# q, k and v as interleaved Strassen quads at the front of an attention and gMLP kernel, with all of v at one time

## The chip, the cores and the metric

The kernel runs on one core of a Trainium2 chip. The metric is the device time of one execution in microseconds (us), as the median of several executions. Every run told here was in the fast state. PE is the TensorE matmul engine, DVE is VectorE, ACT is ScalarE, SP is SyncE (which here issues nearly all transfers), POOL is GpSimd. "Granted clock" is the share of its full speed at which TensorE was clocked.

## The reference, cut to what matters

```python
def _A_ref(x, wqkv, wo):                     # S = 2048, D = 1024, H = 32 heads of 32
    W, dil = (8, 2)                          # each position attends to 8 others, two apart
    qkv = (x @ wqkv).reshape(B, S, 3, H, Dh).transpose(2, 0, 3, 1, 4)
    ...
    logits = einsum('bhsd,bhswd->bhsw', q, kg) * scale      # kg, vg: k and v gathered
    attn = softmax(where(mask, logits, -1e9))
    o = einsum('bhsw,bhswd->bhsd', attn, vg)
    return o.transpose(...).reshape(B, S, D) @ wo

def _B_ref(x, w_in, w_sp, b_sp, w_out):      # gMLP: w_in 1024 x 3584, w_sp 2048 x 2048
    z = gelu(x @ w_in);  z1, z2 = halves of z;  z2 = layernorm(z2)
    g = einsum('ts,bsf->btf', w_sp, z2) + b_sp
    return (z1 * g) @ w_out

g = sigmoid((x * gate_w).sum(-1))
return g * _A_ref(x, A_wqkv, A_wo) + (1 - g) * _B_ref(x, ...)
```

## The kernel before

PE works through these stages: transposes of x and the first quarter of z2 (to 35 us), q, k and v with the rest of z2 (to 288 us), then z1, the spatial product and the output product. The 32 heads are eight groups of four. For each group PE makes q and k in eight direct tiles of eight matmuls, and then the band products, q times k near the diagonal. ACT copies the bands out, SP stores them to memory (`band_d`) and loads the 8 logits of every position back (`att_L`), DVE takes the maxima and subtracts them, ACT applies exp, DVE normalises and weighs v. v goes through memory too (`v_d`), because each position needs v of other positions.

```python
def qk_tile(g, t, c):                        # direct: 8 matmuls of 512 columns
    ps = low_bank()                          # one of banks 0 to 3
    for kt in range(KT):
        nc.tensor.matmul(ps[:], w[:, t, kt, :], xT[:, kt, 512 * c:512 * (c + 1)], ...)
    note(nc.scalar.copy(dst[...], ps[:]...))           # counted: evacuation number n

def attend1(g):                              # logits: load, maxima, subtract, exp
    for e in range(2):
        sync.dma_start(L[:, 256 * e:256 * e + 256]..., band_d[g] ...)
    tt(att_m[:], L4[:, :, 0:4, :], L4[:, :, 4:8, :], ALU.max)
    ...
    last_sub[0] = tt(L4, L4, att_m[:, :, 0:1, :].to_broadcast(...), ALU.subtract)
    exps[g] = nc.scalar.activation(L[:], L[:], ACT.Exp, ...)
    # its place in ACT's order: behind evacuation number EXP_AFTER[g]

def weigh(g, e, after=None):                 # half a group: 4.42 + 4.28 us of DVE
    tt(prod..., v_t ..., att_A ..., ALU.mult)
    tt(p3[:, 0:4, :], p3[:, 0:4, :], p3[:, 4:8, :], ALU.add)
    ...                                      # two more additions

for g in range(NG):                          # the main loop
    main = []
    if g == 1: main += [v_tile(0, j) ...]    # first half of v: 16 direct tiles
    if g + 1 < NG: main += [qk_tile(g + 1, t, c) ...]
    else: main += [z2_tile(i, c, low_bank) ...]
    if g == 3: main += [v_tile(1, j) ...]    # second half of v
    ...                                      # three band_sets of g between the tiles (banks 4 to 7)
    if g == 1: load_v(0); weigh(0, 0)
    if g > 0: load_v(g)
    attend1(g)
    if g > 0: weigh(g - 1, 1, last_sub[0])
    attend2(g)                               # sum, reciprocal, att_A
    if g > 0: weigh(g, 0)
```

The later stages use Strassen quads (seven block products in place of eight), two of them interleaved product by product, one on banks 0 to 3 and one on banks 4 to 7. Partial results move from bank to bank by copies, and later products add onto them:

```python
def strassen(A11, A12, A22, S1, ..., T4, vs, c11, c12, c21, c22, share=nc.scalar.copy):
    product(X, zip(A11, B11), True);   nc.scalar.copy(Y[:], X[:])
    yield
    product(V, zip(S1, T1), True);     share(vs, V[:])          # S, T: sums of blocks, by DVE
    yield
    product(Y, zip(S2, T2), False);    nc.scalar.copy(Z[:], Y[:])
    ...                                # products X, Y, Z, V; c22(Y), c12(Z) are DVE additions
```

The order of the instructions on an engine is fixed when the kernel is built. A "NoSync dependency" in the code below fixes such an order without any semaphore.

## Time and profile before

| | before |
|---|---|
| median of 3 runs | 681.91 us (681.83 to 683.17) |
| profiled run | 682.25 us, span 680.2, granted clock 0.999 |
| PE, DVE, ACT busy | 98%, 60%, 43% |
| chain that ended last | PE 95%, DMA 2%, DVE 1% |
| weighing on DVE starts | 102.38 us |
| DVE starts the x differences for z1 | 287.08 us |
| z1 starts on PE (its refresh matmuls: four that write whole banks ahead of the quads that add onto copies in them; 0.86 us in the chain, and no run tried those quads without them) | 288.02 us |
| PE idle for ACT, DVE or a DMA, 30 to 305 us | 0.24 us |

The views themselves, and what is read from them, stand in the prediction below.

### The profile page before, as it was taken

How to read it: one execution, taken by the hardware profiler on the slowest of the kernel's cores; microseconds unless marked ns; L12 is line 12 of the kernel's file. 1: busy time of each engine (PE TensorE's matmuls, PEld its weight loads, DVE VectorE, ACT ScalarE, POOL GpSimd, SP SyncE). 2: the span in 40 equal slices, each digit the busy share in tenths (PEclk: the TensorE clock that was granted, in tenths of full speed). 3: DMA queues.
4: the chain of work that ended last, by engine and by line, in shares of the span. 5: the costliest groups of instructions: out<-in, count | busy, mean ns of one | idle time of the engine just before them, and what ended most of it. 6: DMA issues, size and time to landing. Idle time of an engine off the chain costs nothing.

```text
span 680.2 us, 10313 instructions
## 1 busy us (share of the span) xinstructions
PE 665.4 (98%) x4075; PEld 323.0 (47%) x4135; DVE 407.4 (60%) x551; ACT 289.5 (43%) x547; POOL 6.1 (1%) x15
## 2 busy tenths in 40 slices
PE   6999999999999999999999999999999999999997
PEld 3544654466444555544444444444444444444443
DVE  1000119899199989866769766888676695333301
ACT  4435634624566889677866311212112122222221
POOL 1000000000000000000100000000000000000000
PEclk9999999999999999999999999999999999999999
DMA  9995654764666470138894587648356299944100
GB/s 232 225 277 116 139 137 116 167 172 94 155 177 154 126 163 1 52 104 191 210 187 155 140 195 153 151 129 255 95 149 167 67 208 187 212 106 98 46 32 31
DMA packets 241743, 98.12 MB, mean 144 GB/s; under 512 B 189712, under 2 KB 235168, under 8 KB 241696
## 3 DMA queue, kind: packets, MB, share of 16 engines
q1 hardware_dynamic: 241008, 96.94, 58.2%
q8 instruction: 32, 0.52, 0.3%
q10 hardware_dynamic: 688, 0.53, 0.2%
q14 instruction: 15, 0.12, 0.1%
HBM read 45.10 MB, written 36.61 MB: 120 GB/s over the span
## 4 chain that ended last, share of the span: by engine, by line
PE 95%; DMA 2%; issue 1%; DVE 1%; SPq 1%; ACT 0%; ACTq 0%; DVEq 0%
PE psum_all L474 56%; PE psum_all L272 16%; PE psum_all L232 15%; PE psum_all L280 6%; PE psum_all L312 2%; DMA band_d_71<-arena 1%; DMA arena<-in_A_x_dram 1%; SPq L184 0%; DMA arena<-o_d 0%; DMA v_d<-arena 0%; PE psum_all L202 0%; DVE arena L685 0%; ACT arena L283 0%; DVE arena L680 0%; DVE arena L525 0%
## 5 line engine op out<-in xcount | busy, mean ns | idle before, releaser
L474 PE MATMUL psum_all<-arena 128*128 128x512 f16 (+1 forms) x1758 | 385.6, 379 | 2.0 <-DVE arena L685 0.2
L474 PEld LDWEIGHTS <-arena 128*128 128x128 f16 (+1 forms) x1792 | 175.3, 98 | 212.2 <-issue 1.3
L272 PE MATMUL psum_all<-arena 128*128 128x512 bf16 x493 | 111.0, 379 | 2.3 <-issue 1.9
L232 PE MATMUL psum_all<-arena 128*128 128x448 bf16 (+1 forms) x512 | 99.7, 355 | 0.0
L365 DVE TENSOR_TENSOR arena<-arena,att_A 128x8192 f16<-128x8192 bf16 x16 | 70.7, 4420 | 12.1 <-DMA arena<-v_d 12.0
L272 PEld LDWEIGHTS <-arena 128*128 128x128 bf16 x512 | 48.6, 98 | 56.8 <-issue 0.2
L232 PEld LDWEIGHTS <-arena 128*128 128x128 bf16 x512 | 49.8, 98 | 47.0 <-issue 1.5
L365 DVE TENSOR_TENSOR arena<-arena 128x4096 f16<-128x4096 f16 (+2 forms) x48 | 67.3, 1401 | 1.2
L274 ACT CAST arena<-psum_all 128x512 bf16<-128x512 f32 x64 | 37.4, 586 | 53.3 <-PE psum_all L272 53.3
L280 PE MATMUL psum_all<-arena 128*128 128x512 bf16 x249 | 55.4, 379 | 0.9 <-issue 0.4
L483 ACT COPY psum_all<-psum_all 128x512 f32<-128x512 f32 x36 | 20.5, 570 | 80.7 <-PE psum_all L474 80.7
L523 DVE TENSOR_TENSOR arena<-arena 128x512 f16<-128x512 bf16 (+2 forms) x37 | 20.7, 568 | 42.1 <-PE psum_all L474 30.9
L234 ACT ACTIVATE arena<-psum_all 128x448 bf16<-128x448 f32 x64 | 34.7, 547 | 26.2 <-PE psum_all L232 26.0
L280 PEld LDWEIGHTS <-arena 128*128 128x128 bf16 x256 | 36.7, 144 | 18.5 <-issue 0.5
L497 ACT COPY psum_all<-psum_all 128x512 f32<-128x512 f32 x36 | 20.6, 571 | 48.7 <-PE psum_all L474 48.6
L490 ACT COPY psum_all<-psum_all 128x512 f32<-128x512 f32 x36 | 20.5, 570 | 48.6 <-PE psum_all L474 48.3
L590 ACT ACTIVATE arena<-psum_all 128x512 bf16<-128x512 f32 x56 | 31.6, 599 | 7.2 <-DVE psum_all L593 3.7
L319 ACT CAST arena<-psum_all 128x1988 f16<-128x1988 f32 (+1 forms) x24 | 33.7, 1405 | 1.1 <-PE psum_all L312 0.4
L526 DVE TENSOR_TENSOR arena<-arena 128x512 f16<-128x512 bf16 (+2 forms) x37 | 20.6, 566 | 21.2 <-PE psum_all L474 15.5
L338 DVE TENSOR_TENSOR att_m<-att_L_106 128x256 f16<-128x256 f16 x4 | 1.2, 290 | 50.8 <-DMA att_L_106<-band_d_68 32.8
L283 ACT CAST arena<-psum_all 128x512 bf16<-128x512 f32 x32 | 18.4, 587 | 26.5 <-PE psum_all L280 25.9
L487 ACT COPY arena<-psum_all 128x512 f32<-128x512 f32 x22 | 12.8, 587 | 34.5 <-PE psum_all L474 33.7
(87 smaller groups left out, 361.5 us busy)
## 6 DMA issues: line engine op xcount, KB each, us to landing
arena<-v_d SPq DMA_DIRECT2D x8, 960.0 KB, 6.9
z_d<-arena SPq DMA_DIRECT2D x28, 256.0 KB, 2.6
arena<-z_d SPq DMA_DIRECT2D x28, 256.0 KB, 3.3
zg_d<-arena SPq DMA_DIRECT2D x56, 128.0 KB, 2.2
arena<-zg_d SPq DMA_DIRECT2D x32, 224.0 KB, 3.1
arena<-in_A_wqkv_dram SPq DMA_DIRECT2D x16, 256.0 KB, 5.6
v_d<-arena SPq DMA_DIRECT2D x32, 128.0 KB, 2.4
o_d<-arena SPq DMA_DIRECT2D x4, 1024.0 KB, 5.5
```

Source lines behind the costliest of these rows:

```text
L232: nc.tensor.matmul(ps[:, 0:N], xT[:, kt, i * P:(i + 1) * P], w2[:, kt, w2_off[c]:w2_off[c] + N], start=(kt == 0), stop=(kt == KT - 1))
L234: inst = nc.scalar.activation(z2[:, i, ZC * c:ZC * (c + 1)], ps[:, 0:ZC], ACT.Gelu_apprx_tanh, accum_out=s1[:, 4 * i + c:4 * i + c + 1])
L272: nc.tensor.matmul(ps[:], w[:, t, kt, :], xT[:, kt, 512 * c:512 * (c + 1)], start=(kt == 0), stop=(kt == KT - 1))
L274: inst = nc.scalar.copy(dst[:, :, 256 * c:256 * (c + 1)], ps[:].rearrange("p (n e) -> p e n", e=2))
L280: nc.tensor.matmul(ps[:], _sub_ap(xT_flat, kt * S + j, [[NJ, P]]), wv[:, kt, 512 * hf:512 * hf + 512], start=(kt == 0), stop=(kt == KT - 1))
L319: evac = nc.scalar.copy(dst, src)
L365: inst = nc.vector.tensor_tensor(*a)
L474: nc.tensor.matmul(bank[:], lhsT, rhs, start=(start and m == 0), stop=(stop and m == n - 1), skip_group_check=True)
L497: seed = nc.scalar.copy(V[:], Y[:])
L523: first = nc.vector.tensor_tensor(s_out[0], a21, a22, ALU.add)
L526: nc.vector.tensor_tensor(s_out[2], a11, a21, ALU.subtract)
L590: last_gelu[0] = nc.scalar.activation(z1s[:, f, a, :], bank[:], ACT.Gelu_apprx_tanh)
```

## The change

The intent: 40 fewer matmuls. q and k of groups 0 and 1 become four quads, and 24 of the 32 v tiles become six quads, all at the front, on all eight banks. For that, all of v is made at one time (before: halves in groups 1 and 3), the x differences that the quads need go to buffers that attention uses later, and the places of the exps are counted anew. The eight v tiles of the first two row sets (j = 0 and 1) stay direct, to carry the six band sets of groups 0 and 1 between them.

```diff
-    EXP_AFTER = (20, 27, 51, 60, 83, 93, 103, 117)
+    EXP_AFTER = (7, 10, 22, 33, 43, 53, 65, 78)
...
+    front_x_sums()                       # x differences for the front, on DVE
+    qk_sums(0)
+    refresh([bank_roles[r][y] for r in range(2) for y in (1, 2)])
+    run(qk_quad(0, 0), qk_quad(0, 1))
+    qk_sums(1)
+    run(qk_quad(1, 0), qk_quad(1, 1))
+    wv_sums()
...
+    for m, args in enumerate(tiles):     # 8 direct v tiles, j = 0 and 1
+        for n in range(6):
+            if (0, 1, 3, 4, 5, 7)[n] == m:
+                band_set(n // 3, n % 3)  # bands of group 0, then of group 1
+                if n == 2:
+                    attend1(0)
+        v_tile(*args)
+    refresh(bank_roles[1][1:3])
+    for j in (2, 4, 6):
+        run(v_quad(j), v_quad(j + 1))
+    load_wqk(4, sync.dma_start)
+    for t in range(2):
+        for c in range(4):
+            qk_tile(2, t, c)
+    load_v(0)
+    attend2(0)
+    weigh(0, 0)
+    load_v(1)
+    attend1(1)                           # logits of group 1: maxima, exp
+    weigh(0, 1, last_sub[0])
+    attend2(1)
+    weigh(1, 0)
+    for g in range(2, NG):               # as before, without v
...
```

In the new quads `share` is a DVE copy, so DVE serves each quad with one copy and two additions.

## The prediction

> **What bounds the kernel now.** I read first the page's busy shares, slices and groups.
>
> ```profile
> PE 665.4 (98%) x4075; PEld 323.0 (47%) x4135; DVE 407.4 (60%) x551; ACT 289.5 (43%) x547; POOL 6.1 (1%) x15
> ...
> PE   6999999999999999999999999999999999999997
> ...
> DVE  1000119899199989866769766888676695333301
> ...
> L272 PE MATMUL psum_all<-arena 128*128 128x512 bf16 x493 | 111.0, 379 | 2.3 <-issue 1.9
> ...
> L280 PE MATMUL psum_all<-arena 128*128 128x512 bf16 x249 | 55.4, 379 | 0.9 <-issue 0.4
> ```
>
> TensorE (PE) is busy 98% of a 680.2 us span, 9 or more tenths in every slice but the ends. VectorE (DVE) idles up to about 102 us (zeros and ones, but for one slice), then runs at 8 to 9 tenths. The two groups are the q/k tiles (L272, 64 tiles of 8 matmuls) and the v tiles (L280, 32 of 8). A share of busy time can hide waits, so next what PE waited for, and the chain that ended last:
>
> ```profile
> PE psum_all L202 <- DMA arena<-in_A_x_dram: 5.8, 2, 3.5
> ...
> PE psum_all L280 <- ACT arena L283: 0.2, 1, 0.2
> ```
> ```profile
> 225.90 62.28 PE psum_all L232 x328
> 288.18 0.86 PE psum_all L635 x4
> 289.10 12.03 PE psum_all L474 x55
> 301.18 12.03 PE psum_all L474 x55
> ```
>
> PE loses 5.8 us to the first x loads and hardly anything afterwards; the chain is matmuls back to back. From 289.10 to 301.18 two interleaved seven-product quads (the layer's z1 stage) run: 56 matmuls in 12.08 us, 0.2157 us each. So the existing quads of four matmuls a product already run at PE's full rate with ScalarE (ACT) and DVE serving them. A matmul removed on this path is worth 0.2157 us, provided that nothing else takes its place. The candidate is DVE, whose timeline I read next (start, length, instruction, in brackets the idle time before):
>
> ```profile
> 90.20 0.23 DVE L355 TENSOR_TENSOR att_r<-att_s,g_att 128x64 f16<-128x64 f32 x1
> 102.38 4.42 DVE L365 TENSOR_TENSOR arena<-arena,att_A 128x8192 f16<-128x8192 bf16 x1 [11.96 <-DMA arena<-v_d]
> ...
> 187.65 0.29 DVE L338 TENSOR_TENSOR att_m<-att_L_106 128x256 f16<-128x256 f16 x1 [15.20 <-DMA att_L_106<-band_d_72]
> ...
> 280.46 4.28 DVE L365 TENSOR_TENSOR arena<-arena 128x4096 f16<-128x4096 f16 x3
> 287.08 4.63 DVE L563 TENSOR_TENSOR arena<-arena 128x2048 f16<-128x2048 bf16 x4 [2.35 <-PE psum_all L232]
> ```
>
> The weighing of v (L365) begins when v has come back from memory, at 102.38, and ends about 284.7; DVE waits 2.35 us and starts at 287.08 on x differences for z1, which need the end of the z2 tiles on PE (288.2). So attention on DVE ends with only 2.4 us to spare. Its idle stretches between 102.38 and 284.74, added from this view, are 2.80 + 0.75 + 15.20 + 0.86 + 0.68 + 0.78 = 21.1 us; its work there is 182.4 - 21.1 = 161.3 us, of which about 5.0 us are sums for z1.
>
> [...] before, four full ones stand at 288.18 and take 0.86 us. [...]
>
> ```profile
> L365 DVE TENSOR_TENSOR arena<-arena,att_A 128x8192 f16<-128x8192 bf16 x16 | 70.7, 4420 | 12.1 <-DMA arena<-v_d 12.0
> ...
> L593 DVE TENSOR_TENSOR psum_all<-psum_all,arena 128x512 f32<-128x512 f32 x28 | 18.0, 694 | 10.9 <-ACT psum_all L497 10.9
> ...
> L563 DVE TENSOR_TENSOR arena<-arena 128x2048 f16<-128x2048 bf16 x8 | 9.4, 1221 | 2.3 <-PE psum_all L232 2.3
> ```
>
> 2048 columns from SBUF take 1.22 us, 512 from PSUM 0.69 us.
>
> **The change, part by part.**
>
> PE, removed. q and k of two groups: 16 tiles of 8 matmuls = 128 become 4 quads of 7 products of 4 = 112. v of six blocks: 24 tiles of 8 = 192 become 6 quads of 28 = 168. Together 40 matmuls, 40 x 0.2157 = 8.6 us, all on the path.
>
> PE, added. Two further refreshes, 4 and 2 matmuls, in strips of 32 rows on different parts of the array, so that they may overlap: at most 6 x 0.22 = 1.3 us, my estimate 0.8. The hand-overs between bank users cost more. The tiles rotated through four banks while band products (q times k near the diagonal) used the other four. Now a band set follows a quad on banks 4 to 7 and waits for the quad's last copy (0.59 us plus signalling), a first quad product follows a direct tile on the same bank, and the six band sets of two groups are squeezed between eight tiles. A band evacuation takes 1.82 us on ACT and a tile 1.73 us on PE, so adjacent sets can wait some tenths. I choose 2.3 us for all this. PE so reaches the end of z2 at 288.2 - 8.6 + 0.8 + 2.3 = 282.7 us.
>
> The start. The first quads need wqk of group 0 (issued at 22.9, landing in about 5.6) at 35.3 and the first x difference 1.7 us later. The x differences are 8 x 1.22 = 9.8 us on a DVE that idles from 16 to 36.8 us, and the last x transposes are issued by 22.8 and land in about 4. Only the third difference has a catch: its buffer covers the zeros that are stored to v's border in memory, the last of the start-up loads, whose issue ends at 36.1; it may start near 40 and end at 42.7. Its product comes after eight others of the interleaved pair, at about 42. I count no wait.
>
> ACT and DVE in the quads: per quad of 28 x 0.2157 = 6.04 us ACT has five copies of 0.57 to 0.59 = 2.9 us, DVE three of 0.69 = 2.1 us; over ten quads DVE gets 21 us, and 9.8 us of x differences, 8 x 0.42 = 3.4 of weight sums of q and k and 4 x 1.22 = 4.9 of v. These 39 us lie before 116 us, where DVE had nearly nothing. Beside PE, free.
>
> Moved: all v at one time. From 35.3: four quads 24.2 + 1 us refresh and hand-over, eight direct v tiles 13.8, six band sets 3.7, hand-overs 1.5, six quads 36.2: v is complete at about 115.7 us. Before, its first half was at 94.5:
>
> ```profile
> 94.52 0.59 ACT L283 CAST arena<-psum_all 128x512 bf16<-128x512 f32 x1 [1.14 <-PE psum_all L280]
> 95.13 2.06 SPq L184 DMA_DIRECT2D v_d<-arena  x4
> ...
> 97.30 0.96 SPq L184 DMA_DIRECT2D arena<-v_d  x2
> ```
>
> There the last copy ended at 95.1, small stores (128 KB each) followed, and weighing began 7.3 us after. Now the last store is 1 MB, then the first load of v of 960 KB: at some 200 GB/s (what the page's GB/s row shows in busy slices) 5 us each plus about 1.3 us of issue and latency each, 12.5 us. Weighing begins at 115.7 + 12.5 = 128 us, 26 us later than before. The second v phase inside group 3 disappears, and with it the waits of DVE for group logits (15.2 of the 21.1 us): the logits of groups 2 to 7 now come every 8 x 1.73 + 1.9 = 15.7 us, faster than DVE's 20 us per group. DVE is thus busy without a gap from 128 to 128 + 161.3 = 289.3 us.
>
> The sum. PE is ready for z1 at 282.7, DVE with everything at 289.3. The first z1 products that need a late x difference start some 3.5 us into z1, so at about 287 with 1.22 us of DVE before it. If all attention work stood before those differences, PE would wait about 4 us; but they have a high priority, and part of the last weighing (8.6 us) can come after. It would then be caught up inside z1, where DVE is busy 63.2 of 86 us. I put PE's wait at a third of the full one plus some friction from 4.4 us instructions in front of the quads' additions: 1.0 us. Total: 681.9 - 8.6 + 0.8 + 2.3 + 1.0 = 677.4 us.
>
> **Rivals.**
>
> First: DVE becomes the bound at the join. For it speak 289.3 against 282.7; against it the 27% idle share of DVE in z1. If the queue's order puts all weighing ahead, or v returns 3 us later than thought, PE waits 4 to 7 us and the time is 681 to 684; the gain is gone.
>
> Second: ACT's exps stall PE. They stand at fixed places in ACT's order, and ACT already waited 5.4 us for DVE once (at 148 us), which cost PE only 0.24 us as three more banks were free. With DVE further behind, a wait of 8 us or more would cost PE 3 us at a time in several groups: 684 or more. Against it: the differences of logits that an exp needs are short and come ahead of the weighing in DVE's order.
>
> Third: everything stays hidden and hand-overs cost as little as before: 681.9 - 8.6 + 0.8 = 674.
>
> Fourth: the quads at the front stall for the zeros' store or for wqk: 2 to 4 us more, 680.
>
> **Range and chances.** The gain is capped near 8 us, 1.2%; for 2% (668.3) there are no matmuls. A loss of 2% (695.5) would need several stalls at once. I take 672.8, the third rival with a little luck, to 683 for the first. Faster by over 2%: 0.02; within 2%: 0.95; slower by over 2%: 0.03.
>
> **What would show it.** PE matmul count down by some 34, refreshes counted; the quads at the front taking 12.1 us a pair; weighing beginning near 128 us and running with no gap over 1 us; the end of z2 near 282.7; then the number to look for, PE's wait for DVE in the first z1 pair, about 1 us, and leftover weighing inside z1. It would be wrong if PE stalls in the front's quads, if exps hold ACT for over 6 us, or if z1 starts more than 3 us late.

## The result

The kernel after took 690.22 us (median of 4, 689.39 to 693.58; a fifth fast run, 690.55, counts in the ratio). Before had a median of 682.54 us over 4 runs, the three of the table above and one of 686.91. The ratio is 1.0107, with a 95% interval of 1.0061 to 1.0154; the width comes mostly from that fourth run (against it alone the ratio would be 1.006, against the first three 1.012). Ratios here are the mean time of one kernel's fast runs over that of the other's fast runs of the same rounds, so not quite the ratio of the medians. By the 2% rule the class is "same", as given 95 chances in 100, but the time lies 12.8 us above the prediction and outside the range.

The page of after: busy shares, then the slices of PE, DVE and of the granted clock, then the chain by engine.

```profile
PE 670.4 (97%) x4101; PEld 319.0 (46%) x4101; DVE 441.0 (64%) x601; ACT 292.3 (42%) x557; POOL 6.2 (1%) x15
...
PE   6999969999899999999999999999999999999997
...
DVE  1562223299999998995678966789684694333301
...
PEclk9999989999899999999999999999999999999999
...
PE 78%; DVE 9%; DMA 8%; ACT 3%; issue 1%; SPq 1%; ACTq 0%; DVEq 0%
```

PE is still at 97%, but a slice near 95 us now stands at six and one near 181 us at eight, and in both the clock stands at eight. The chain has lost 17 points from PE (95% before): DVE has 9%, DMA 8%, ACT 3%. The weight loads, of which every matmul has one (4101 of each in after), fell from 4135 to 4101, the 34 predicted. (The 4075 matmuls of before are the records that were not missing.) So the matmuls are saved, and something else was lost. What PE waited for, in after (us in total, times, longest):

```profile
PE psum_all L281 <- DVE arena L423: 5.5, 1, 5.5
PE psum_all L440 <- ACT arena L442: 3.2, 1, 3.2
PE psum_all L237 <- ACT arena L239: 1.6, 1, 1.6
PE psum_all L475 <- ACT arena L482: 0.9, 1, 0.9
```

Before, this view had no wait longer than 0.2 us except for the first loads. Now 11.1 us stand here, half of it in one wait: 5.5 us of a v quad for a DVE addition (L423). The chain of after around it shows where the 5.5 us come from (start, length, what):

```profile
79.90 4.46 DMA band_d_69<-arena
...
84.38 0.56 SPq L189
...
85.69 4.53 DMA band_d_69<-arena
...
90.27 2.44 DMA att_L_107<-band_d_69
...
93.61 0.43 DVE att_L_107 L504
94.04 0.61 DVE arena L423
...
94.69 6.27 PE psum_all L281 x15
```

Read it upward. PE resumed at 94.69 because DVE's addition for a bank ended at 94.65. That addition followed the subtraction of group 1's maxima, which followed the maxima, which waited for the logits of group 1. Those landed at 92.71: their second load was issued at 90.27, once a band store had landed that SP had not issued before 84.98, because the first load stood ahead of it in SP's queue and waited for an earlier band store. DVE's own timeline says the same (start, length, instruction; in brackets the idle time before):

```profile
92.80 0.29 DVE L501 TENSOR_TENSOR att_m<-att_L_107 128x256 f16<-128x256 f16 x1 [7.10 <-DMA att_L_107<-band_d_69]
...
93.96 0.68 DVE L423 TENSOR_TENSOR arena<-psum_all,arena 128x512 bf16<-128x512 f32 x1
...
137.84 4.42 DVE L528 TENSOR_TENSOR arena<-arena,att_A 128x8192 f16<-128x8192 bf16 x1 [3.94 <-DMA arena<-v_d]
...
290.27 4.43 DVE L528 TENSOR_TENSOR arena<-arena,att_A 128x8192 f16<-128x8192 bf16 x1
...
298.93 4.62 DVE L675 TENSOR_TENSOR arena<-arena 128x2048 f16<-128x2048 bf16 x4
```

DVE stood idle for 7.10 us in front of maxima that nobody needed yet (their exp had its place behind evacuation 10, in group 2's tiles, after 120 us), while the addition that PE was waiting for stood four places behind. The trace shows DVE keeping to its order: the addition ran at 93.96, directly behind the subtraction of 93.61, though PE had been idle, and so done with its product, since 89.23 (94.69 less 5.46).

The last three lines are the second thing to see: weighing begins at 137.84, not at the predicted 128, and from it to the x differences for z1 at 298.93 it is 161.1 us, of which DVE idles for 2.97. Predicted were 161.3 us without a gap. So the length was right, and the start was 9.8 us late.

The third thing is what a PE stall costs beyond itself. Stretches of after (start and end; length; busy us of PE, PEld, DVE, ACT, POOL with counts; granted clock; DMA share; GB/s):

```profile
94.70:98.00 3.30, 3.30 (x8) 1.29 (x8) 0.69 (x1) 1.07 (x2) 0.00 (x0) 0.50 0.00 0
98.00:102.00 4.00, 4.00 (x14) 2.00 (x13) 0.84 (x2) 0.29 (x1) 0.00 (x0) 0.69 0.00 0
...
186.90:190.40 3.50, 3.50 (x10) 0.99 (x9) 3.50 (x3) 3.12 (x4) 0.00 (x0) 0.50 0.00 0
```

After the stall the clock was 0.50 until about 100.5 (0.50 x 3.3 us, then 0.69 over 4 us, which is 2.5 us at half speed). Half speed for 5.8 us is a further 2.9 us, behind 5.46 us of idling. The same again at 186.89 (0.50 over 3.5 us, then 0.68 over the next 3.6), after an idle time of only 3.15 us, which came from an exp that had waited for DVE (ACT's and PE's timelines of after):

```profile
185.74 0.63 ACT L505 ACTIVATE att_L_107<-att_L_107 128x512 f16<-128x512 f16 x1 [8.97 <-DVE att_L_107 L504]
```

```profile
186.89 3.57 PE L440 MATMUL psum_all<-arena 128*128 128x512 bf16 x8 [3.15 <-ACT arena L442]
```

So an 8.97 us wait of ACT cost PE 3.15 us, and then eight matmuls took 3.57 us instead of 8 x 0.2157 = 1.73.

PE itself did not wait for DVE at z1 in this kernel: it came there at 299.67, 17.0 us after the predicted 282.7, and DVE had begun the x differences at 298.93. Its own losses make up nearly all of the 17.0: 5.46 and some 2.6 us in v's stage, 5.6 us of waits for ACT behind it, and 2.9 us of half clock there. Whether those waits are a cause of their own is what e2 and e3 ask.

From z1 on nothing has changed: the time less the start of z1 is 693.58 - 299.67 = 393.9 us in the traced run of after and 682.25 - 288.02 = 394.2 in before.

The traced run (693.58) is the slowest of the five, with a granted clock of 0.990; the others had 0.994 to 0.997. One half-clock stretch of 5.8 us is 2.9 / 690 = 0.004 of the mean clock, so I take it that the others had about one such stretch less; they have no trace, so that is argued and not shown.

### The profile page after: what moved, and what is told of

Its sections match the earlier page's. It is cut to its first block, busy times and chain, and to the rows that moved or that the text cites. A ratio compares the mean times of both kernels' runs of the same rounds, so it can differ in the third digit from the quotient of the medians.

```text
span 691.8 us, 10361 instructions
## 1 busy us (share of the span) xinstructions
PE 670.4 (97%) x4101; PEld 319.0 (46%) x4101; DVE 441.0 (64%) x601; ACT 292.3 (42%) x557; POOL 6.2 (1%) x15
## 4 chain that ended last, share of the span: by engine, by line
PE 78%; DVE 9%; DMA 8%; ACT 3%; issue 1%; SPq 1%; ACTq 0%; DVEq 0%
PE psum_all L281 63%; PE psum_all L237 11%; DVE arena L528 7%; PE psum_all L440 2%; DMA band_d_69<-arena 1%; ACT arena L239 1%; DMA band_d_74<-arena 1%; PE psum_all L448 1%; DMA band_d_71<-arena 1%; DMA arena<-v_d 1%; DMA arena<-in_A_x_dram 1%; DMA band_d_68<-arena 1%; ACT arena L244 1%; DMA v_d<-arena 1%; ACT arena L482 1%
## 5 line engine op out<-in xcount | busy, mean ns | idle before, releaser
L281 PE MATMUL psum_all<-arena 128*128 128x512 f16 (+1 forms) x2072 | 452.6, 381 | 5.8 <-DVE arena L423 5.5
L281 PEld LDWEIGHTS <-arena 128*128 128x128 f16 (+1 forms) x2072 | 210.3, 102 | 246.6 <-issue 12.4
L237 PE MATMUL psum_all<-arena 128*128 128x448 bf16 (+1 forms) x512 | 100.5, 356 | 1.6 <-ACT arena L239 1.6
L440 PE MATMUL psum_all<-arena 128*128 128x512 bf16 x384 | 88.9, 387 | 3.2 <-ACT arena L442 3.2
L237 PEld LDWEIGHTS <-arena 128*128 128x128 bf16 x512 | 50.0, 99 | 48.9 <-issue 3.8
L291 ACT COPY psum_all<-psum_all 128x512 f32<-128x512 f32 x46 | 26.2, 570 | 87.2 <-PE psum_all L281 83.1
L440 PEld LDWEIGHTS <-arena 128*128 128x128 bf16 x384 | 36.9, 99 | 47.5 <-issue 6.7
L305 ACT COPY psum_all<-psum_all 128x512 f32<-128x512 f32 x46 | 26.3, 571 | 61.5 <-PE psum_all L281 61.4
L298 ACT COPY psum_all<-psum_all 128x512 f32<-128x512 f32 x46 | 26.2, 570 | 59.3 <-PE psum_all L281 58.9
L331 DVE TENSOR_TENSOR arena<-arena 128x512 f16<-128x512 bf16 (+3 forms) x40 | 22.6, 575 | 44.9 <-PE psum_all L281 30.9
L442 ACT CAST arena<-psum_all 128x512 bf16<-128x512 f32 x48 | 27.3, 589 | 24.8 <-PE psum_all L440 24.8
L335 DVE TENSOR_TENSOR arena<-arena 128x512 f16<-128x512 bf16 (+3 forms) x40 | 22.6, 574 | 23.3 <-PE psum_all L281 13.5
L334 DVE TENSOR_TENSOR arena<-arena 128x512 f16<-128x512 f16 (+3 forms) x40 | 22.6, 575 | 7.9 <-PE psum_all L281 7.5
L295 ACT COPY arena<-psum_all 128x512 f32<-128x512 f32 x22 | 12.8, 586 | 34.3 <-PE psum_all L281 33.6
L705 DVE TENSOR_TENSOR psum_all<-psum_all,arena 128x512 f32<-128x512 f32 x28 | 18.0, 693 | 10.1 <-ACT psum_all L305 10.1
L903 DVE TENSOR_TENSOR arena<-psum_all,arena 128x512 bf16<-128x512 f32 x8 | 5.5, 690 | 29.0 <-ACT psum_all L305 29.0
L336 DVE TENSOR_TENSOR arena<-arena 128x512 f16<-128x512 bf16 (+3 forms) x40 | 22.3, 572 | 1.7 <-PE psum_all L281 1.6
```

The source lines that it names most:

```text
L237: nc.tensor.matmul(ps[:, 0:N], xT[:, kt, i * P:(i + 1) * P], w2[:, kt, w2_off[c]:w2_off[c] + N], start=(kt == 0), stop=(kt == KT - 1))
L281: nc.tensor.matmul(bank[:], lhsT, rhs, start=(start and m == 0), stop=(stop and m == n - 1), skip_group_check=True)
L291: last_seed[0] = nc.scalar.copy(Y[:], X[:])
L305: seed = nc.scalar.copy(V[:], Y[:])
L331: first = nc.vector.tensor_tensor(s_out[0], a21, a22, ALU.add)
L442: inst = nc.scalar.copy(dst[:, :, 256 * c:256 * (c + 1)], ps[:].rearrange("p (n e) -> p e n", e=2))
```

## The experiments

Theory at this point: (1) group 1's maxima, put ahead of the v quads' additions in DVE's order, cause the stall, and by it the late v. (2) The exps' waits are not a cause of their own: from the start of weighing, DVE's 161 us chain sets the end, and the exps only hand its lateness on to PE. Rivals: the exps are simply placed too early, and placing them later gives the time back; or the v quads themselves cost more than the matmuls they save.

All eleven kernels (there is no e6) gave the reference's result. They ran in four jobs on four chips. Before took 686.05 to 687.71 us (medians) there, some 5 us more than in three of its first four runs, with a wide spread (683 to 692). There is no trace of before from these chips, and the cause stays open. So a kernel is compared with before by its ratio, and with others of its job by either; after itself was not run there, and a comparison with its 1.0107 may be off by some tenths of a per cent. Intervals are given in brackets. The expectations of e1 to e4 are in us and reckon with before's 681.91; divided by it, they are ratios of 0.9987 to 1.0023 (e1), 1.0089 to 1.0133 (e2), 0.9928 to 0.9987 (e3) and 1.0016 to 1.0060 (e4).

### e1_logits_behind: group 1's maxima behind the last v quad addition

```diff
+        if g == 1:
+            tc.add_manual_dep(top.ins, last_vadd[0].ins.name, NOSYNC, ...)   # top: the first maximum
```

> Only the order on VectorE is changed: the softmax maxima of group 1 go behind the additions of the v quads. My theory (the chain that sets the end is: v complete, v stored and loaded, 161 us of attention on VectorE without a gap, then z1): the 5.5 us wait of PE for a VectorE addition at 89 to 95 us disappears and so does the half clock after it, weighing begins near 128 instead of 137.8 us, the z2 tiles end near 290 instead of 299.7 us, time 681 to 683.5. Rival (the quads themselves are slow, by their strided operands and hand-overs): the wait moves to another instruction, the six v quads still take over 44 us, time stays 688 to 691.

Measured: 686.58 us, ratio 0.9985 (0.9975 to 0.9994). PE's timeline of after, for comparison, then PE's and DVE's timelines of this kernel:

```profile
94.69 25.93 PE L281 MATMUL psum_all<-arena 128*128 128x512 f16 x105 [5.46 <-DVE arena L423]
```

```profile
80.20 32.27 PE L281 MATMUL psum_all<-arena 128*128 128x512 bf16 x145
...
118.20 12.03 PE L443 MATMUL psum_all<-arena 128*128 128x512 bf16 x54
```

```profile
130.45 4.42 DVE L533 TENSOR_TENSOR arena<-arena,att_A 128x8192 f16<-128x8192 bf16 x1 [4.72 <-DMA arena<-v_d]
```

The v quads run from 80.20 on without a stall, in 39.0 us from their first matmul (79.16) to the first one behind them (118.20), against 47.2 in after (79.18 to 126.36); the 8.1 us between are the 5.46 of waiting and about 2.6 at half clock. Weighing starts 7.4 us earlier. The ratio is 1.2% lower, 8.3 us; by the times themselves, from other chips, it is 3.6 us. In us the expectation was missed (681 to 683.5); as a ratio 0.9985 lies at its edge (0.9987). Theory 1 is shown: one edit of DVE's order took away the stall, the half clock (1.00 granted from 79 to 118.2 us) and 7.4 us of the start. But the gain over before is 0.15%, where the 34 matmuls alone are worth 1.1%: PE still waits for exps in the middle groups (2.41 and 3.25 us the longest) and weighing starts 2.4 us later than even predicted.

### e2_exps_late: the exps of groups 2 to 7 later

```diff
-    EXP_AFTER = (7, 10, 22, 33, 43, 53, 65, 78)
+    EXP_AFTER = (7, 10, 31, 41, 51, 62, 75, 88)
```

> Only the places of the exps of groups 2 to 7 on ScalarE are moved 8 to 10 evacuations later, so that ScalarE doesn't stand waiting for VectorE's differences. My theory (VectorE's chain is the bound, the exps only hand its lag to PE early): PE's waits for ScalarE (3.2, 1.6 and 0.9 us and the half clock behind the first) vanish, but weighing still begins near 137 us and ends near 299 us, and PE waits at the start of z1 instead, 4 to 7 us: time 688 to 691, unchanged. Rival (the exps' places cost the time by themselves): 682 to 684.

Measured: 695.93 us, ratio 1.0121 (1.0100 to 1.0143), not faster than after. PE's timeline of this kernel:

```profile
293.69 0.39 PE L349 MATMUL psum_all<-arena 32*128 32x512 bf16 x3
...
301.88 1.04 PE L281 MATMUL psum_all<-arena 128*128 128x512 f16 x4 [3.68 <-DVE arena L675]
305.29 14.89 PE L281 MATMUL psum_all<-arena 128*128 128x512 f16 x57 [2.37 <-DVE arena L675]
```

PE comes to z1 6 us earlier than in after (293.69 against 299.67), because the waits of tiles for ACT have shrunk to below 1 us each. It then loses those 6 us in two waits for the x differences, which DVE starts at 300.61, behind all of the weighing. The ratio is the expected one. So placing the exps later gives nothing back while DVE is late: theory 2, against the first rival.

### e3_both: e1 and e2 together

```diff
+ the two edits above
```

> Both edits together. My theory: weighing begins near 128 us and ends near 289 us; PE ends z2 near 284 us and then waits some 1 to 4 us for VectorE in the first z1 pair; time 677 to 681, at or a little under the kernel before (682). Rival of the strided quads: 686 or more. Rival that the two stalls simply add up and VectorE is no bound: 674 to 676.

Measured: 688.19 us, ratio 1.0008 (0.9995 to 1.0021), a miss: on the same chip it is slower than e1. PE reaches z1 at 284.97, 7.3 us before e1, and then waits 4.03 and 1.52 us for the x differences, at half clock in between and after (0.50 from 293.5 to 295.4 us and from 296.9 to 299.0). DVE starts those at 292.23, 1.0 us later than in e1, and has been idle for 1.15 us more before it. So the 7.3 us are gone soon: at 310.2 us PE has loaded the weights of 76 matmuls of z1, in e1 of 81. Freeing PE is worthless here; only an earlier end of DVE's chain would help.

### e4_v_direct: the six v quads as direct tiles again

```diff
-    wv_sums()
...
-    refresh(bank_roles[1][1:3])
-    for j in (2, 4, 6):
-        run(v_quad(j), v_quad(j + 1))
+    for j in range(2, 8): ...                        # 24 direct tiles: 192 matmuls for 168
+                v_tile(j, half, n)
-    EXP_AFTER = (7, 10, 22, 33, 43, 53, 65, 78)
+    EXP_AFTER = (19, 26, 46, 57, 67, 77, 89, 102)
```

> All of v stays at one time, but as direct tiles: 24 more matmuls, no v quads, no sums of v weights; q and k of groups 0 and 1 stay quads. 24 x 0.2157 = 5.2 us more of PE. My theory: no VectorE addition can stall v, so v is complete near 120.5 us (the changed kernel: 126 to 127), weighing begins near 131.5 us and ends near 292.5 us; time 683 to 686, faster than the changed kernel in spite of more matmuls. Rival (the move of v, not a stall in it, costs everything): 689 or more.

Measured: 688.69 us, ratio 1.0023 (1.0012 to 1.0035). With 24 more matmuls, 5.2 us, this kernel is no slower than after (688.69 against 690.22 us, and lower in ratio); no tile of v waits for DVE now. Against e1, where the quads run without the stall, it is slower by 0.38%, 2.6 us on the same chip. So the second rival falls: with the stall gone the v quads gain, about half of what their matmuls are worth, as these two kernels stand (PE idles for 6.9 us in e4 and for 10.1 in e1). In us the time misses the expectation, as a ratio it lies within. But with 16 matmuls fewer than before and no stall in v, e4 is still not faster than before: weighing starts at 131.47 where it started at 102.38, which points to a price of making v at one time, with or without the stall. No run kept v in its two halves beside the quads of q and k.

### e5_k1_behind_v: group 1's q and k behind v, direct

```diff
-    EXP_AFTER = (7, 10, 22, 33, 43, 53, 65, 78)
+    EXP_AFTER = (7, 25, 35, 45, 55, 66, 79, 91)
-    qk_sums(1)
-    run(qk_quad(1, 0), qk_quad(1, 1))
...                                                   # bands of group 0 alone between the v tiles
+    for t in range(2): ... qk_tile(1, t, c)          # behind the v quads
     load_v(0)
     attend2(0)
     weigh(0, 0)
+    weigh(0, 1)
...                                                   # then qk_tile(2, ...) with the bands of group 1
```

> q and k of group 1 go behind v, as direct tiles (8 more matmuls each... together 16 tiles' worth less 56: 8 more matmuls, 1.7 us of PE); the two weighings of group 0 no longer wait for group 1; exps placed for that order. v is then complete near 102 us and stored and loaded while PE works on group 1. My theory (the time is the start of weighing plus its 161 us, when that is later than PE's own end): weighing begins near 113 us, VectorE idles some 5 to 10 us for the logits of group 1 near 130 us and ends near 285 us, PE ends z2 near 285 us, both together; ratio to before 0.990 to 0.995. Rival (quads on strided x differences cost as much as they save): ratio 0.998 or more.

Measured: 691.79 us, ratio 1.0089 (1.0055 to 1.0124), a miss. (Group 1's q and k are 64 matmuls as direct tiles and 56 as quads, hence the 8 more.) Weighing starts at 116.05, 21.8 us before after's. But DVE then idles for 20.90 us, in five waits for logits (7.62 and 5.64 us the longest), and starts z1's x differences at 299.74, later than in after. An early start is no gain if the next group's logits are not there.

### e7_split_store: e1, with v's stores of groups 0 and 1 first

```diff
-        for half in range(2):
-            ... sync.dma_start(dst, vst_blocks[...])            # 512 KB, all groups
+        for g0, g1 in ((0, 2), (2, NG)):
+            for half in range(2):
+                ... sync.dma_start(dst, vst_blocks[...][:, g0:g1])
```

> The first experiment (maxima of group 1 behind the v additions) with each v store split by groups, groups 0 and 1 first, so that the first load of v waits for 256 KB and not for 1 MB. My theory: weighing begins 2 to 4 us earlier than in the first experiment (130.5 us) and the time falls by as much: ratio to before 0.993 to 0.996 (first experiment: 0.9985). Rival (PE's own time is the bound by now): no change, 0.998 to 0.999.

Measured: 687.34 us, ratio 1.0012 (0.9998 to 1.0025), a miss. Weighing starts at 127.13, 3.3 us before e1's, and the time is not better. DVE idles for 9.54 us instead of 2.58; the longest wait is 4.06 us for the logits of group 3, at 178.32. The chain of this kernel from group 2's logits to that wait:

```profile
156.18 1.81 ACT arena L486
...
158.03 0.64 PE psum_all L479 x56
...
168.39 4.76 DMA band_d<-arena
...
173.21 5.09 DMA att_L<-band_d
```

It is a ring. The exp of group 2 had waited 4.65 us on ACT; the next band copy (L486) stood behind it in ACT's order; the next band products (L479) had to wait for it, 1.79 us; and the bands of group 3, stored and loaded back in 9.9 us, were late on DVE, whose lateness holds the next exp (9.37 us) and then PE (4.75 us). SP's order adds to it: a band copied out by 161.2 was stored at 165.29 only, behind a load of logits (163.97) and the store of o (164.62), which waits for DVE's weighing.

### e8_k1_behind_split: e5 with that split

```diff
+ the edits of e5 and the split of e7
```

> Group 1 behind v, and the split stores, together. Weighing of group 0 begins 2 to 4 us earlier than without the split, but then VectorE waits for the logits of group 1 anyway, so my theory expects no further gain over group 1 behind v alone: the same ratio within 0.002. Rival (any earlier start of weighing counts): 0.003 to 0.005 lower.

Measured: 691.18 us, ratio 1.0062 (1.0040 to 1.0083), 0.0027 below e5: more than the theory's 0.002, less than the rival's 0.003, and the intervals overlap, so this run decides nothing. DVE idles for 21.89 us between the first and the last weighing.

### e9_pool_queue and e10_split_pool: v's loads and o's stores from GpSimd

```diff
-        sync.dma_start(v_t, ...)
+        (sync if g < 2 else nc.gpsimd).dma_start(v_t, ...)
-            sync.dma_start(dst, obuf)
+            nc.gpsimd.dma_start(dst, obuf)
```

e9 is this on e1; e10 is this on e7.

> The first experiment (maxima of group 1 behind the v additions) with the stores of o and the loads of v from group 2 on issued from GpSimd's queue instead of SyncE's. In SyncE's in-order queue these wait for VectorE's weighing and hold up the band stores and logit loads behind them. Theory of the queue: PE's waits for ScalarE (3.6, 3.2 and 2.1 us in the first experiment) shrink to under 4 us together; but VectorE's chain stays, weighing from 130.5 us on without idle time, so the time falls only by the 3 us of idle time of VectorE: ratio to before 0.994 to 0.998. Rival (the queue does not matter): 0.998 to 0.9995.

> The same with split v stores. Weighing begins near 127 us. Theory of the queue: the idle time of VectorE for logit loads that appeared with the split stores (9.5 us in five waits) goes under 3 us, weighing and the sums end near 290 us, ratio to before 0.991 to 0.996. Rival (logits come late for another reason, PE and ScalarE): idle time stays at 6 us or more, ratio 0.998 to 1.002.

Measured: e9 686.26 us, 1.0003 (0.9984 to 1.0021); e10 686.75 us, 1.0002 (0.9984 to 1.0021); both misses, with times in or next to the rivals' ranges. In e10 DVE's idle time is down from e7's 9.54 us to 5.75 and z1's x differences start at 291.76 instead of 295.42. But in both kernels PE still loses 8 to 9 us to waits for ACT, the longest 4.18 and 4.30 us, each behind an exp that had waited some 9 us for DVE (8.80 and 8.92), and the 16 matmuls behind each took 5.22 and 5.30 us instead of 16 x 0.2157 = 3.45. In e9 the clock there was 0.50 for 1.87 us and 0.65 over the next 2.00, some 3.3 us at half. So PE is now later than DVE. That the exps' places, which were counted for other starts, are to blame is argued: no run moved them in these two kernels.

### e11_k1_behind_pool: e8 with the GpSimd queue

```diff
+ the edits of e8 and of e9's queues
```

> Group 1 behind v, split stores, and the GpSimd queue. Without the queue VectorE idled some 30 us between 133 and 240 us for logit loads. Theory of the queue: this falls to the 6 to 10 us before the logits of group 1, attention ends near 283 us and PE's own end of z2, near 285 us, sets the time: ratio 0.988 to 0.994. Rival (the late bands of group 1 themselves): 1.000 or more.

Measured: 684.69 us, ratio 0.9974 (0.9956 to 0.9993): faster than e8 by 0.9%, though less than hoped. (Against e1's 0.9985 the intervals overlap.) DVE's idle time is 16.70 us (21.89 in e8, and not the some 30 that the expectation names), and PE's waits for ACT are 4.7 us in all, one of 2.63 in front of the bands at 145.89, behind ACT's exp of group 1, whose logits came late (DVE waited 9.42 us for them).

### e12_exps_moved: e11 with two exps moved

```diff
-    EXP_AFTER = (7, 25, 35, 45, 55, 66, 79, 91)
+    EXP_AFTER = (7, 28, 35, 45, 57, 66, 79, 91)
```

> The last kernel (group 1 behind v, split v stores, GpSimd queue) with two exps placed later on ScalarE: that of group 1 by three evacuations, that of group 4 by two, as ScalarE stood 5.5 and 2.3 us before them waiting for VectorE and PE waited 2.6 and 0.7 us for ScalarE. PE is the bound there by my reading (z2 ends at 291 us with attention not yet done, and z1 starts without a wait), so the time should fall by about 3 us: ratio to before 0.992 to 0.995. Rival (VectorE's chain still bounds it): ratio unchanged near 0.997, with the wait showing up at the start of z1.

Measured: 681.32 us (6 runs) against 686.52 for before on the same chip, ratio 0.9931 (0.9908 to 0.9953), as expected. It beats before on its chip, and by ratio also after. PE's wait for DVE in this kernel:

```profile
PE psum_all L281 <- DVE arena L681: 0.5, 1, 0.5
```

This is the only wait for DVE up to z1 (a later one is of 0.2 us), and none for ACT is above 0.52 us; z1 starts at 285.67 and DVE starts its x differences at 289.36; PE has to wait for them 0.46 us. By the ratio on one chip the prediction's gain, 677.4 / 681.9 = 0.9934, is there, with eight matmuls more than in after. Against the trace of before, from another chip, z1 starts 2.35 us earlier (285.67 against 288.02).

### All in one table

Weighing and x differences: start on DVE. DVE idle: between the first and the last weighing multiplication. PE idle: for ACT, DVE or a DMA from 30 to 310 us. All from the one traced run of each kernel.

| kernel | ratio to before | weighing | DVE idle | x differences | z1 on PE | PE idle |
|---|---|---|---|---|---|---|
| before | 1 | 102.38 | 21.07 | 287.08 | 288.02 | 0.2 |
| after | 1.0107 | 137.84 | 2.97 | 298.93 | 299.67 | 11.3 |
| e1 | 0.9985 | 130.45 | 2.58 | 291.20 | 292.23 | 10.1 |
| e2 | 1.0121 | 138.93 | 3.63 | 300.61 | 293.69 | 14.5 |
| e3 | 1.0008 | 130.50 | 3.73 | 292.23 | 284.97 | 8.1 |
| e4 | 1.0023 | 131.47 | 4.93 | 295.16 | 294.81 | 6.9 |
| e5 | 1.0089 | 116.05 | 20.90 | 299.74 | 298.14 | 9.7 |
| e7 | 1.0012 | 127.13 | 9.54 | 295.42 | 293.98 | 9.2 |
| e8 | 1.0062 | 115.71 | 21.89 | 300.39 | 296.51 | 9.8 |
| e9 | 1.0003 | 130.78 | 3.38 | 292.15 | 293.18 | 8.2 |
| e10 | 1.0002 | 126.67 | 5.75 | 291.76 | 292.79 | 8.9 |
| e11 | 0.9974 | 115.30 | 16.70 | 294.12 | 290.88 | 4.7 |
| e12 | 0.9931 | 114.93 | 12.59 | 289.36 | 285.67 | 2.5 |

Two columns together carry the times: PE needs the first x difference about 4.3 us after it begins z1 (its first one, of 1.2 us, ends at "x differences" plus 1.2), and it needs to be there itself. In e2, e3, e8 and e12 DVE is the later of the two, and PE waits for it there; in e11 they come within 0.1 us of each other and PE doesn't wait; in the other changed kernels PE is the later, held by waits for ACT, the longest of them behind exps that DVE or the logits kept back (in after by the stall in v's stage too).

What is not told apart: in the step from e1 to e12 the order of group 1, the split stores, GpSimd's queue and the exps' places come in one after another. Alone, group order (e5) loses, and the split (e7) and the queue on e1 (e9) gain nothing. On top of each other, e8 to e11 (the queue) and e11 to e12 (two exps) gave 0.9% and 0.4%, each from a different chip.

## Why the prediction was wrong

**The matmuls.** Right: 34 fewer, and the quads of q and k took 25.7 us (35.77 to 61.49) where 24.2 + 1 were counted; v quads were to begin near 79.5 and began at 79.18. Of the first four refreshes, in strips of 32 rows, three took 0.39 us together (35.77); the four of before, over 128 rows, had taken 0.86. The doubts about the start (x differences, zeros, weights of group 0) were unfounded, as the prediction had it; rival four is out.

**"ACT and DVE in the quads ... Beside PE, free."** This is the step that failed first. It added up DVE's work (39 us in a nearly idle stretch) and not its order. One instruction in front of the additions that waits for a transfer (7.10 us here) made them all late, however little DVE had to do. v's stage, counted at 36.2 us, took 47.9 (79.18 to the last addition's start at 126.34 and 0.69 of its own). The 11.7 us more are 5.46 of waiting, about 2.6 of half clock, 1.5 for seven matmuls of group 2's tiles that were drawn in between, 0.4 of refresh, and as the rest some 1.7 of hand-overs with the last addition. e1 shows the first two.

**"Weighing begins at 115.7 + 12.5 = 128 us."** It began at 137.84: v complete at 127.0 instead of 115.7, and the way through memory 10.8 us instead of 12.5 (4.59 for v's store to land, 5.54 for the load, 0.7 between). Even e1, without the stall, starts at 130.45.

**"DVE is thus busy without a gap from 128 to 128 + 161.3 = 289.3 us."** The length was right (161.1 us, 2.97 of them idle); the end moved with the start, to 298.93.

**"I put PE's wait at a third of the full one plus some friction: 1.0 us."** Wrong by its order: in every trace read there the weighing stood in front of the x differences, all of it or (e2, e3) all but a last addition of 0.7 us, so the wait is the full one. In after itself PE was so late that it didn't wait there at all. Where PE was early the wait measured 6.0 us (e2) and 5.5 us (e3), not 1. This is the first rival, sized there at 4 to 7 us and given too little weight.

With these two terms put right, the prediction's own sum is 677.4 - 1.0 + 4 + 9.8 = 690.2 us, against a measured 690.22. The closeness is luck, as the traced run was 3.4 us slower than that, and as in after PE lost the time before z1 and not by waiting there. But e2 and e3 show that DVE's chain, by its start and its place in front of z1, sets about the same end when PE is early.

**The second rival** was there too: ACT's waits of 8.97 us (group 3), 5.01 (group 4) and 4.63 (group 2) for DVE. The prediction had a wait of 8 us cost PE 3 us; 8.97 cost 3.15, and about as much again through the clock, which the prediction did not count. But e2 and e3 show that in this kernel it is not a loss of its own: take it away, and the wait for DVE comes back at z1.

**Range and chances.** The class was right. The range ended at 683 because it let DVE be 3 us late at most, and the stall in the quads was not among the rivals: rival four thought of loads and zeros at the front, not of DVE's order. All three of its signs of being wrong came: PE stalled in the front's quads (5.46 us), an exp held ACT for 8.97 us, and z1 started 17.0 us late.

**A slip in the reading.** "Zeros and ones, but for one slice": the six slices up to 102 us have no exception. The one slice that differs is the eleventh, a one (170 to 187 us), among the eights and nines that follow. Nothing rests on it.

## What to carry to other kernels

An engine that is idle 40% of the time can still be late (DVE, 60% busy before and 64% after, held PE for 5.46 us): look not only at how much work a change gives it but at what stands in front of that work in its fixed order, above all instructions that wait for a transfer. When a long chain on one engine ends where another engine needs it, its start is what counts, and moving the places where its lateness shows gains nothing (e2, e3), until the chain itself ends early enough (e12). The same holds for the engine that issues transfers: there a transfer that waited for one engine held back the ready transfers of another (in e7 a band copied out by 161.2 us was stored at 165.29), and a second issuing queue parted them. It helped in e11 (ratio 0.9974, against 1.0062 in e8) and not in e9 (1.0003, against 0.9985 in e1), where PE was held by something else.

## What the stalls and the second queue came to

- The clock behind a stall: in after, stalls of 5.46 and 3.15 us left it at half for about 5.8 us each, 2.9 us of further loss; in e4 and e9 (stalls of 4.69 and 4.18 us) half speed lasted 3.2 to 3.3 us. The length of the stall alone did not tell what followed: 3.15 us in after was followed by half clock, 3.25 us in e1 was not (1.00 behind it), and in e5 the clock stayed at 0.98 for 1.4 us after a stall of 3.82 us and only then fell to 0.50, with PE busy. What decides it, these traces do not show.
- The second queue: it parted transfers that waited for different engines. From e8 to e11 DVE's idle time fell from 21.89 to 16.70 us and the ratio from 1.0062 to 0.9974 (on e1 the same edit, e9, gained nothing).
- The order on an engine: one 7.10 us wait of DVE for a transfer became 5.46 us of PE and, with the clock, 8.1 us of v's stage.
